# Block sums of the second layer's weights: made early and kept in DRAM instead of made where they are used

## The chip, the core and the metric

The kernel runs on one core of one Trainium2 chip. The metric is the device time of one execution in microseconds (us), lower is better. TensorE does the matrix products, VectorE and GpSimd elementwise work, ScalarE activations, copies and casts; SyncE and ScalarE start the transfers.

## The reference

Softcapped attention, followed by a two-layer network on its rows. All inputs and the output are float32.

```python
batch, n_heads, seq, head_dim = (4, 12, 448, 64)
scores = scale * np.matmul(q, k.transpose(0, 1, 3, 2))
scores = cap * np.tanh(scores / cap)
attn = softmax(scores)
x = np.matmul(attn, v)              # rows: 1792 x 768
h = x @ w_in                        # 768 x 2048
g = np.maximum(0.01 * h, h)
out = g @ w_out                     # 2048 x 768
```

(`softmax` stands for the reference's subtraction of the maximum, exponential and division by the sum.)

## The kernel before

The 1792 tokens are cut into runs of 256, 512, 512 and 512 columns. Attention goes head pair by head pair. The first two runs go through both layers as plain products, unit by unit (`plan_unit`, 34 units for each run: 16 of layer 1, then 18 of layer 2, a third of one block of 128 output columns each), while attention of later pairs is still running. The last two runs are taken together, as the two halves of a 2x2 block product with seven products in the place of eight (Winograd's form): layer 1 in eight "duos" of seven products of nine matmuls (`plan_duo`, L968), layer 2 in 7 x 3 products of 24 matmuls (`plan_product`, L1158). A float32 operand is split into a large and a small part: ScalarE or VectorE casts (L271, L275), VectorE or GpSimd subtracts (L278), and TensorE multiplies large by large, large by small, small by large.

The seven products need, of the blocks A11, A12, A21, A22 of the weights, A11, A12, A22 themselves and four sums:

```python
S1 = A21 + A22        # product 5
S2 = S1 - A11         # product 6
S3 = A11 - A21        # product 7
S4 = A12 - S2         # product 3
```

In layer 2 they are made when their turn comes, in the order `SECOND = (1, 5, 6, 7, 3, 2, 4)`, for each of three pairs p of output blocks and each half hf of the inner blocks. `plan_weights2` loads halves (256 KB) of the float32 weights, that an earlier stage left in the DRAM tiles `scratch2`, with `load_half` (L1074) into a ring of places in SBUF, and adds them with `tt2` (through `tt`, L832); S1 and S2 are kept in six places `s_home`, S3 and S4 are made in the place of the load. The finished sum is split for TensorE.

A product that adds to another's result stays in its PSUM bank. After products 1, 6 and 7 the bank is copied (L271, `keep_sum` in a duo) before the next product adds to it; after product 5 VectorE adds the bank into the output's block (L978 in a duo, L1178 in layer 2), and then product 3 adds to the bank. The banks `sc` lie in pairs in one PSUM tile (`sc_0`, `sc_1`).

The order is made by a planner (`Plan.issue`): each step has a rank, a cost per engine that may do it and the things it reads and writes. The planner takes, of the steps that are ready, the one that could begin first, then the one of lowest rank. The table `T` holds offsets by which ranks are shifted. Each engine executes its steps in the order that results, and so does each transfer queue. `raws` is the SBUF place into which the keys and queries of a quad of heads are loaded before they are transposed (`kraw`, `qraw`; L475 to L478); block operands of the last stage (`places("raws")`) take it over.

Of the kernel before, what the change touches and what calls it, by code (L numbers as in the profile page):

```python
# [9 lines left out]
F32 = mybir.dt.float32  # L10
# [45 lines left out]
    run=[576.75],
    duo=[2.07, 284.05, 910.86, -136.23, -111.69, -95.43, -23.8, -31.91],
    last=[435.37, -538.07, 227.36, -1.68, 128.15, -1225.57, -129.94, 128.6, 69.02, 131.52, 2.55, 130.66, 136.38, -656.66, 129.2, -205.76, 732.75, 763.07, -47.84, 258.93, 422.61],
    side=[-652.13, -774.99, 249.82, -374.78, 381.42, 60.8, -562.89, -191.96, 172.13, 34.67, 371.92, 318.88, -250.01, -353.24, 417.43, -547.36, -373.61, -914.07, -815.49, -153.64, -2.66, 402.24, -370.85, -380.79, -52.61, 520.81, -342.53, -165.1, -770.54, 713.99, -143.3, 356.82, -878.93, -458.23, 282.61, -767.29, 427.25, -70.55, 928.25, 302.12, -692.1, 9.97, 304.17, -205.4, -109.08, 907.85, 369.95, -402.59, -925.39, 395.77, 496.96, 41.15, 846.93, -1216.73, 1505.94, -22.9],
    phases=[(1000000000.0, {'pe': 25.03, 'dve': 0.49, 'pool': 0.13})],  # L60
# [111 lines left out]
def softcap_attention_mlp(  # L172
# [951 lines left out]
    def plan_product(idx, p, rank):  # L1124
# [58 lines left out]
        if i == 2:  # L1183
            cost, engines = {"sp": 2.1}, [nc.sync, nc.scalar]
# [150 lines left out]
```

## Time and profile before

| | us |
|---|---|
| median of three runs | 647.86 (647.61 to 649.33) |
| the profiled execution's own time | 649.59 |
| its span, first to last instruction | 647.7 |
| TensorE busy | 624.6 (96%) |
| VectorE busy | 522.3 (81%) |
| ScalarE busy | 345.6 (53%) |
| GpSimd busy | 99.2 (15%) |

The profile is one execution. An engine's busy time is what its instructions took; matmuls overlap, so a matmul's own duration (0.39 us) is longer than the step from one to the next (2.04 us for nine). Plain products and attention fill the time up to about 400 us, the duos the time to about 523 us, layer 2 of the last runs the rest up to 638.8 us, where TensorE ends; the last stores follow. Lines are those of the kernel before. In the changed kernel they are some lines further down: L278 becomes L283, L565 L570, L832 L865, L968 L1001, L1158 L1168.

### The profile page before, as it was taken

The numbers are of one execution on the slowest core, as the hardware profiler recorded it, in microseconds if no ns is written. First come the engines' busy times: TensorE is split into PE (matmuls) and PEld (weight loads), VectorE is DVE, ScalarE is ACT, GpSimd is POOL, SyncE is SP. The second block draws the span as 40 slices with busy tenths as digits, with TensorE's granted clock in tenths as the row PEclk, the third lists the DMA queues.
The fourth block names the chain that finished last, engine by engine and source line by source line (L and its number), as shares of the span: only waits on it lengthen the run. The fifth ranks groups of instructions, "written<-read, shape, count | busy, mean of one in ns | idle before, by whom it ended". The sixth has DMA issues, their size and how long they took to land.

```text
span 647.7 us, 9153 instructions
## 1 busy us (share of the span) xinstructions
PE 624.6 (96%) x3220; PEld 433.5 (67%) x3220; DVE 522.3 (81%) x834; ACT 345.6 (53%) x524; POOL 99.2 (15%) x86
## 2 busy tenths in 40 slices
PE   7899999999999999999999999999998999999994
PEld 4333655555666568677665788778887778877884
DVE  4899999999899989468675997664779999998851
ACT  4998688976867754445446244223433634564320
POOL 1032202301030322000120402010221200101100
PEclk8999999999999999999999999999999999999998
DMA  8964568859749754223232155210311275246444
GB/s 276 368 214 139 156 215 294 253 163 297 237 129 329 231 155 148 97 58 122 72 91 54 48 122 122 79 49 1 97 50 40 73 254 157 71 132 146 90 73 70
DMA packets 105254, 93.49 MB, mean 144 GB/s; under 512 B 53745, under 2 KB 84465, under 8 KB 105201
## 3 DMA queue, kind: packets, MB, share of 16 engines
q1 hardware_dynamic: 98496, 91.58, 47.6%
q10 hardware_dynamic: 6704, 1.25, 1.0%
q8 instruction: 27, 0.44, 0.3%
q14 instruction: 27, 0.21, 0.1%
HBM read 74.71 MB, written 18.09 MB: 143 GB/s over the span
## 4 chain that ended last, share of the span: by engine, by line
PE 92%; DVE 3%; ACT 3%; DMA 1%; issue 1%; SPq 0%; ACTq 0%
PE m L743 34%; PE sc L968 11%; PE sc L1158 10%; PE sc L499 9%; PE po L544 9%; PE po L1158 5%; PE po L968 4%; PE sc L496 3%; PE m L1158 3%; PE m L968 2%; PE po L519 1%; DMA raws<-in_k_dram 1%; ACT exps L554 1%; PE m L548 1%; PE po L591 1%
## 5 line engine op out<-in xcount | busy, mean ns | idle before, releaser
L743 PE MATMUL m<-bank,ws 128*128 128x256 f32 x384 | 91.6, 388 | 0.0
L271 ACT CAST w<-ws 128x384 fp32r<-128x384 f32 (+3 forms) x84 | 52.0, 626 | 71.3 <-PE m L743 19.8
L743 PEld LDWEIGHTS m<-bank,ws 128*128 128x128 f32 x384 | 70.2, 190 | 25.1 <-issue 12.2
L554 ACT ACTIVATE exps<-sc 128x896 f32<-128x896 f32 (+1 forms) x72 | 58.4, 835 | 43.1 <-PE sc L499 21.9
L278 DVE TENSOR_TENSOR w<-ws,w 128x384 fp32r<-128x384 f32 (+3 forms) x85 | 62.1, 736 | 21.4 <-ACT w L271 20.2
L499 PE MATMUL sc<-heads 32*128 32x448 f32 x576 | 66.8, 571 | 5.2 <-DVE heads L477 2.4
L743 PE MATMUL m<-bank,w 128*128 128x512 f32 x288 | 68.2, 394 | 0.0
L743 PEld LDWEIGHTS m<-bank,w 128*128 128x128 f32 x288 | 53.3, 188 | 15.8 <-issue 4.8
L557 ACT ACTIVATE exps<-exps 128x896 f32<-128x896 f32 (+1 forms) x72 | 61.0, 871 | 0.5
L743 PE MATMUL m<-xh,w 128*128 128x512 f32 x192 | 61.2, 394 | 0.0
L499 PEld LDWEIGHTS sc<-heads 32*128 32x128 f32 x576 | 27.2, 186 | 34.1 <-issue 14.4
L544 PE MATMUL po<-exps,norm 128*64 128x448 f32 x232 | 49.0, 551 | 0.0
L743 PEld LDWEIGHTS m<-xh,w 128*128 128x128 f32 x192 | 36.0, 188 | 11.1 <-issue 2.9
L278 POOL TENSOR_TENSOR w<-ws,w 128x384 fp32r<-128x384 f32 (+3 forms) x14 | 20.2, 1440 | 136.4 <-ACT w L271 84.7
L743 PE MATMUL m<-xl,w 128*128 128x512 f32 x96 | 37.4, 390 | 0.0
L544 PEld LDWEIGHTS po<-exps,norm 128*64 128x64 f32 x232 | 14.9, 137 | 29.1 <-issue 21.3
L688 DVE SCALAR_TENSOR_TENSOR bank<-bank 128x768 int32<-128x768 int32 (+1 forms) x34 | 32.5, 960 | 1.8 <-ACT ws L686 1.6
L686 ACT ACTIVATE ws<-bank 128x768 f32<-128x768 f32 (+1 forms) x34 | 29.8, 879 | 6.2 <-PE m L743 4.5
L691 DVE SCALAR_TENSOR_TENSOR ws<-ws,bank 128x768 int32<-128x768 int32 (+1 forms) x34 | 30.3, 896 | 0.3
L1158 PE MATMUL sc<-exps,w 128*128 128x512 f32 x114 | 28.6, 390 | 0.8 <-DVE bank L1178 0.8
L680 ACT ACTIVATE bank<-bank 128x768 int32<-128x768 uint8 (+1 forms) x27 | 23.7, 876 | 5.6 <-DMA bank<-in_moe_w_out_dram 4.2
L1158 PEld LDWEIGHTS sc<-exps,w 128*128 128x128 f32 x114 | 21.3, 188 | 5.6 <-DVE bank L1178 1.2
(229 smaller groups left out, 1186.6 us busy)
## 6 DMA issues: line engine op xcount, KB each, us to landing
ws<-scratch SPq DMA_DIRECT2D x38, 384.0 KB, 3.2
bank<-in_moe_w_in_dram SPq DMA_DIRECT2D x16, 768.0 KB, 7.4
scratch<-ws SPq DMA_DIRECT2D x22, 384.0 KB, 4.3
ws<-scratch SPq DMA_DIRECT2D x28, 256.0 KB, 3.6
raws<-in_k_dram SPq DMA_DIRECT2D x12, 448.0 KB, 5.9
bank<-scratch SPq DMA_DIRECT2D x20, 256.0 KB, 3.6
raws<-in_q_dram SPq DMA_DIRECT2D x11, 448.0 KB, 5.8
norm<-in_v_dram SPq DMA_DIRECT2D x48, 96.0 KB, 3.5
```

Of the source, the lines that this page charges most:

```text
L271: nc.scalar.copy(o, i)
L278: ENG[eng].tensor_tensor(out=o, in0=a, in1=f32(b), op=ALU.subtract)
L499: nc.tensor.matmul(sc[r // 2][:, r % 2, 0:S], keys(a)[part4[r], x, P * g:P * g + P], queries(c)[part4[r], x], **flags)
L544: nc.tensor.matmul(at("po", 2 * i)[half[j], 0:S], at("vc", i)[:, j, g], pf(g)[:, j if wide(g) == 2 else 0], start=(g == 0), stop=(g == NG ...
L554: a = plan.add(r, {"act": ct}, lambda e, sc=sc, g=g: nc.scalar.activation(pf(g), sc(), AF.Tanh, scale=scale_of["tanh"]), vers("sc", [g]) + ...
L557: plan.add(r + 2, {"act": ct + 0.03}, lambda e, g=g: nc.scalar.activation(pf(g), pf(g), AF.Exp, scale=scale_of["exp"]), (), vers("pf", [g] ...
L686: b = plan.add(rank, {"act": ca}, lambda e: nc.scalar.activation(ws(), word(1).bitcast(F32), AF.Abs, scale=2.0 ** -112), [("wr", m)], [("w ...
L688: a = plan.add(rank, {"dve": cv}, lambda e: nc.vector.scalar_tensor_tensor(out=word(1), in0=word(1), scalar=-0x80000000, in1=word(0), op0= ...
L691: plan.add(rank, {"dve": cv}, lambda e: nc.vector.scalar_tensor_tensor(out=z(), in0=z(), scalar=3, in1=word(1), op0=ALU.logical_shift_left ...
L743: nc.tensor.matmul(ps(), l, r, start=begins and some[0] == 0 and i == 0, stop=ends and some[-1] == len(cs) - 1 and i == len(ops) - 1)
L968: nc.tensor.matmul(ps(), l, r, start=start and x == 0, stop=x == len(ops) - 1, skip_group_check=not start)
L1158: nc.tensor.matmul(ps()[:, lo:hi], l, r[:, lo:hi], start=start and n0 == 0 and x == 0, stop=n0 == NK - 2 and x == len(ops) - 1, skip_group ...
```

## The change

The four sums are made in an earlier stage. `plan_sums` is called for 24 cells x: pair p of output blocks (3) and inner block n (8). It loads the four 128x128 blocks of its cell, two at a time, into a third of the raw keys' part of `raws`, makes the four sums in place, and stores the cell to new DRAM tiles `sums2`. The planner may give the additions to VectorE or GpSimd. The cell's loads wait for the last quad's transposes or for the store of the cell three before; the block operands that take `raws` over later wait for the last three cells' stores. `plan_weights2` then has one load of 256 KB per product, pair and half, of a sum from `sums2` or of plain blocks from `scratch2`, and no addition. The places `s_home` are now free, and hold the transposed output of product 2 before its stores, where the ring `ot` did. The table of offsets has new numbers throughout.

```diff
@@ T
+    ps=245,
+    pd=4.5,
...
+    wholes = {}
...
+        wholes[name] = whole
...
+    KEPT = (6, 3, 7, 5)
+    sums2 = [dram.tile([P, 4, 4 * P], F32, name=f"sums2_{s}") for s in range(2 * NPQ)]
+    plan.ring("pre", 3)
...
+    def plan_sums(x, rank):
+        plan.part("sum", "", x)
+        p, n = divmod(x, K4)
+        cell = wholes["raws"][:, 4 * P * (x % 3):4 * P * (x % 3) + 4 * P].rearrange("p (i f) -> p i f", f=P)
+        A11, A12, A21, A22 = ((lambda j=j: cell[:, j]) for j in range(4))
+        freed = [(t, n_quads - 1) for t in ("kraw", "qraw")] if x < 3 else []
+        for row in range(2):
+            e_ = 2 * p + row
+            plan.add(rank - T["wl"], {"sp": 0.65}, lambda e, row=row, e_=e_: nc.sync.dma_start(out=cell[:, 2 * row:2 * row + 2], in_=scratch2[e_][:, n:n + K4 + 1:K4]),
+                     [(f"scratch{NF + NCH * e_ + c}", 0) for c in range(NCH)], [("pr", 2 * x + row)], xfer=0.45, freed=freed if x < 3 else [("pre", x - 3)])
+        cost = {"dve": 0.07 + 1.04e-3 * P, "pool": 0.15 + 2.35e-3 * P}
+        done_ = []
+        for o, a, b, op in ((A22, A21, A22, ADD), (A21, A11, A21, SUB), (A11, A22, A11, SUB), (A12, A12, A11, SUB)):
+            done_ = [tt(rank, o, a, b, op, [("pr", 2 * x), ("pr", 2 * x + 1)], [("pre", x)], cost=cost, after=done_)]
+        plan.add(rank + 2, {"sp": 0.65}, lambda e: nc.sync.dma_start(out=sums2[2 * p + n // 4][:, :, P * (n % 4):P * (n % 4) + P], in_=cell),
+                 [("pre", x)], [("p2", x)], xfer=0.85)
...
+        if name == "raws":
+            over = [("pre", x) for x in range(NF // 2 * NPQ - 3, NF // 2 * NPQ)]
...
-        if i == 5:
-            load_half(1, 0, p, hf, rank, sums, ("S0", s), s_home[s][1])
-            q_, v_ = load_half(1, 1, p, hf, rank)
-            tt2(rank, sums, sums, q_, ADD, [("S0", s), v_], ("S1", s))
-            src, reads = sums, [("S1", s)]
-        elif i == 6:
...
+        if i in KEPT:
+            src, reads = load_half(rank, lambda: sums2[s][:, KEPT.index(i)], [("p2", K4 * p + 4 * hf + k) for k in range(4)])
         else:
...
+            src, reads = load_half(rank, lambda: scratch2[e_][:, lo:lo + 4].rearrange("p c f -> p (c f)"), [(f"scratch{NF + NCH * e_ + c}", 0) for c in range(NCH)])
...
         if i == 2:
-            cost, engines = {"sp": 2.1}, [nc.sync, nc.scalar]
+            cost, engines, ver, freed = {"sp": 2.1}, [nc.sync, nc.scalar], ("oz", 20 + p), s_home[3 + p][1]
+            buf = lambda: s_home[3 + p][0]().rearrange("p (s d) -> p s d", d=32)
...
+    for x in range(K4 * NPQ):
+        plan_sums(x, T["ps"] + T["pd"] * x)
```

What the instructions' order shows, at three places. First TensorE at the end of duo 5 and the start of duo 6 (`po_1` is the bank that duo 5's products 5 and 3 share, `po_0` that of its products 1, 6, 7, 4; `sc_0<-xl` begins duo 6). Before:

```order
L968 MATMUL po_1_82<-exps_2_2530,w_2_1669 128x512 x3
L968 MATMUL po_1_82<-norm_2_2620,w_2_1669 128x512 x6
L968 MATMUL po_0_81<-bank_8_2_2128,w_2_1669 128x512 x3
L968 MATMUL po_0_81<-bank_9_2_2161,w_2_1669 128x512 x4
L968 MATMUL po_0_81<-bank_10_2_2213,w_2_1669 128x512
L968 MATMUL po_0_81<-bank_9_2_2161,w_2_1669 128x512
L968 MATMUL po_1_82<-norm_2_2620,w_2_1669 128x512 x7
```

Now:

```order
L1001 MATMUL po_1_82<-exps_2_2728,w_2_1675 128x512 x3
L1001 MATMUL po_1_82<-norm_2_2803,w_2_1675 128x512 x6
L1001 MATMUL po_0_81<-bank_8_2_2247,w_2_1675 128x512 x3
L1001 MATMUL po_0_81<-bank_9_2_2279,w_2_1675 128x512 x4
L1001 MATMUL po_0_81<-bank_10_2_2368,w_2_1675 128x512
L1001 MATMUL po_0_81<-bank_9_2_2279,w_2_1675 128x512
L1001 MATMUL sc_0_79<-xl_89,w_2_1675 128x512 x9
L1001 MATMUL po_1_82<-norm_2_2803,w_2_1675 128x512 x7
```

Duo 6's first product has moved between the two products on `po_1`.

Second GpSimd during the plain products (L565 and L570, L562 and L567 are softmax sums, L278 and L283 subtractions of splits, L865 the new sums). Before:

```order
L562 TENSOR_TENSOR norm<-exps 128x896
L565 TENSOR_TENSOR norm<-norm,exps 64x448
L278 TENSOR_TENSOR w_1669<-ws,w_1669 128x768
L278 TENSOR_TENSOR raws_1727<-wait,raws_1727 128x512
L565 TENSOR_TENSOR norm<-norm,exps 64x448
L278 TENSOR_TENSOR w_1669<-ws,w_1669 128x768
L278 TENSOR_TENSOR bank_2_1912<-g_103,bank_2_1912 128x512
```

Now:

```order
L567 TENSOR_TENSOR norm<-exps 128x896
L570 TENSOR_TENSOR norm<-norm,exps 64x448 x2
L283 TENSOR_TENSOR w_1675<-ws,w_1675 128x768
L865 TENSOR_TENSOR raws<-raws 128x128 x19
L570 TENSOR_TENSOR norm<-norm,exps 64x448
L865 TENSOR_TENSOR raws<-raws 128x128 x4
L283 TENSOR_TENSOR bank_2_1921<-g_103,bank_2_1867 128x512
L865 TENSOR_TENSOR raws<-raws 128x128 x61
L567 TENSOR_TENSOR norm<-exps 128x896
L865 TENSOR_TENSOR raws<-raws 128x128 x12
```

All 96 additions are on GpSimd, with three other instructions between them.

Third ScalarE at the end (casts of weights `w_2`, and the stores of product 2 from `ot` before, from `norm` now, which ScalarE starts in turn with SyncE). Before:

```order
L271 CAST raws_2_1727<-wait_90 128x512
L271 CAST w_2_1669<-bank_10_3_3594 128x512 x2
L708 DMA out_dram<-ot_0_105 32x4x32 x2
L708 DMA out_dram<-ot_0_105 32x12x32 x2
L708 DMA out_dram<-norm_3_3611 32x4x32 x2
L708 DMA out_dram<-norm_3_3611 32x12x32 x2
```

Now:

```order
L276 CAST raws_2_2600<-wait_90 128x512
L276 CAST w_2_1675<-bank_10_3_3771 128x512
L713 DMA out_dram<-norm_3_3797 32x4x32 x2
L713 DMA out_dram<-norm_3_3797 32x12x32 x2
L276 CAST w_2_1675<-bank_10_3_3771 128x512
L713 DMA out_dram<-norm_3_3797 32x4x32 x2
L713 DMA out_dram<-norm_3_3797 32x12x32 x2
L276 CAST w_2_1675<-bank_10_3_3771 128x512
```

The casts of the last weights now stand behind four stores each.

## Rows read from the trace of the kernel before

**Rows 1.** Five stretches: from:to and length, each engine's busy us, granted clock, DMA share, GB/s.

```profile
core 0: us, PE busy (x) PEld busy (x) DVE busy (x) ACT busy (x) POOL busy (x), PEclk, DMA share, GB/s
...
240.00:360.00 120.00, 120.00 (x600) 83.19 (x600) 84.27 (x117) 56.24 (x81) 15.32 (x9) 1.00 0.31 91
480.00:520.00 40.00, 37.41 (x164) 30.37 (x163) 37.59 (x59) 17.80 (x34) 9.70 (x7) 1.00 0.22 66
520.00:560.00 40.00, 38.49 (x167) 30.94 (x167) 39.34 (x63) 20.26 (x36) 4.09 (x2) 1.00 0.56 171
560.00:600.00 40.00, 38.54 (x169) 31.23 (x168) 36.27 (x62) 19.63 (x36) 2.95 (x2) 1.00 0.51 130
600.00:648.00 48.00, 38.76 (x194) 32.89 (x192) 23.37 (x36) 9.36 (x16) 4.27 (x3) 0.95 0.45 75
```

**Rows 2.** TensorE's waits, 395 to 648 us: for whom, us in total, times, longest.

```profile
PE po L968 <- DVE bank L978: 1.7, 1, 1.7
PE sc L968 <- ACT bank L271: 1.4, 2, 0.7
PE sc L968 <- DVE wait L978: 0.9, 1, 0.9
PE sc L968 <- DVE xh L978: 0.9, 1, 0.9
PE sc L1158 <- DVE bank L1178: 0.8, 1, 0.8
PE sc L1158 <- ACT bank L271: 0.7, 1, 0.7
PE sc L1158 <- DVE wait L978: 0.7, 1, 0.7
```

**Rows 3.** The chain that ended last, 395 to 648 us: start, us, what.

```profile
408.59 0.59 ACT bank L271
...
487.64 2.33 PE po L968 x9
489.97 2.04 PE sc L968 x9
```

**Rows 4.** Line 832, 515 to 610 us: eight of the 24 sums, ns min/median/max.

```profile
L832 DVE TENSOR_TENSOR norm<-norm,ws x8: 680/686/687, 529.2 to 546.2; 128x512 f32<-128x512 f32 x8
```

**Rows 5.** GpSimd's instructions by shape: count, busy us, mean ns, idle before.

```profile
L278 POOL TENSOR_TENSOR w<-ws,w 128x384 fp32r<-128x384 f32 x7 | 8.4, 1196 | 31.2 <-ACT w L271 21.9 <-PE po L968 6.5 <-DMA ws<-scratch 1.4
...
L278 POOL TENSOR_TENSOR xl<-norm,xh 128x192 fp32r<-128x192 f32 x6 | 4.3, 718 | 15.4 <-DVE xh L275 12.7 <-ACT xh L271 2.7
...
L386 POOL MEMSET norm<- 128x128 f32 x2 | 0.3, 205 | 0.0
```

**Rows 6.** Instructions in order of time, 484 to 487 us: start, us, engine, line.

```profile
484.43 1.20 POOL L278 TENSOR_TENSOR w<-ws,w 128x384 fp32r<-128x384 f32 x1 [1.42 <-DMA ws<-scratch]
484.68 1.36 DVE L278 TENSOR_TENSOR w<-g,w 128x384 fp32r<-128x384 f32 x1
...
486.43 0.55 DVE L278 TENSOR_TENSOR w<-ws,w 128x384 fp32r<-128x384 f32 x1
```

**Rows 7.** VectorE's instructions by shape, 240 to 360 us, columns as in Rows 5.

```profile
L278 DVE TENSOR_TENSOR w<-ws,w 128x768 fp32r<-128x768 f32 x16 | 16.7, 1050 | 0.2
...
L278 DVE TENSOR_TENSOR bank<-g,bank 128x512 fp32r<-128x512 f32 x15 | 10.4, 690 | 3.5 <-ACT bank L271 3.2
L565 DVE TENSOR_TENSOR norm<-norm,exps 64x448 f32<-64x448 f32 x7 | 6.2, 893 | 2.7 <-ACT exps L557 2.6
...
L278 DVE TENSOR_TENSOR w<-ws,w 128x640 fp32r<-128x640 f32 x6 | 4.9, 825 | 3.2 <-ACT w L271 2.8
...
L563 DVE TENSOR_TENSOR norm<-norm,exps 128x896 f32<-128x896 f32 x4 | 4.3, 1077 | 0.0
```

**Rows 8.** Instructions in order of time at the end, 618 to 648 us.

```profile
624.59 2.60 ACTq L708 DMA_DIRECT2D out_dram<-ot  x4
...
627.23 0.62 ACT L271 CAST raws<-wait 128x512 fp32r<-128x512 f32 x1 [3.78 <-DMA out_dram<-ot]
...
633.36 9.72 SPq L708 DMA_DIRECT2D out_dram<-norm  x14
...
638.80 0.45 DVE L1167 STREAM_TRANSPOSE norm<-po 128x256 f32<-128x256 f32 x1 [2.15 <-PE po L1158]
```

More of the change, by code (lines that the diff above doesn't have):

```diff
@@ L56 @@
[L56 to L59, printed above, removed]
@@ new lines @@
+    run=[16.57],
+    duo=[330.89, 486.97, 1747.73, -211.67, 48.39, 108.12, 114.85, 478.0],
+    last=[694.33, -552.1, 302.56, 229.54, 261.67, -1251.14, -394.06, -46.46, 1454.11, 271.52, -887.99, 762.71, -422.01, -185.91, 872.64, -981.3, 1478.44, 649.25, -136.75, 640.51, 1013.89],
+    side=[12.81, -328.49, -49.06, -1062.95, 509.42, 262.73, -964.23, -55.46, 439.0, 361.48, 573.73, 395.1, -646.04, -245.17, 769.91, 676.77, 305.52, -862.54, -1734.86, -689.43, 235.24, 495.8, -783.61, -439.02, -267.55, 909.49, -398.82, -193.61, -490.73, 618.92, -471.78, 627.09, -1389.69, -775.61, 401.34, -804.47, 684.13, 380.74, 835.71, 700.02, -796.53, -65.17, 33.36, -58.57, -37.58, 414.87, 723.61, 669.19, -2712.06, 1065.07, -238.9, -713.14, 1524.95, -1959.16, 1872.4, -53.24],
@@ L1069, in softcap_attention_mlp, with load_half @@
     n_loads = [0]
-    s_made = {}
-    tt2 = lambda rank, o, a, b, op, reads, ver, after=(): tt(rank, o, a, b, op, reads, [ver], after=after)
-    def load_half(row, col, p, hf, rank, dest=None, ver=None, freed=()):
-        e_ = 2 * p + row
-        if dest is None:
-            x = n_loads[0]
-            n_loads[0] += 1
-            dest, ver = q_home[x % NQ][0], ("wq", x)
-            freed = [(t, x - NQ) for t in ("wq", "wz")] if x >= NQ else q_home[x][1]
-        lo = NK * col + 4 * hf
-        plan.add(rank - T["wl"], {"sp": 0.65}, lambda e: nc.sync.dma_start(out=dest().rearrange("p (c f) -> p c f", f=P), in_=scratch2[e_][:, lo:lo + 4]),
-                 [(f"scratch{NF + NCH * e_ + c}", 0) for c in range(NCH)], [ver], xfer=0.85, freed=freed)
-        return dest, ver
+    def load_half(rank, source, reads):
+        x = n_loads[0]
+        n_loads[0] += 1
+        dest, ver = q_home[x % NQ][0], ("wq", x)
+        plan.add(rank - T["wl"], {"sp": 0.65}, lambda e: nc.sync.dma_start(out=dest(), in_=source()), reads, [ver], xfer=0.85,
+                 freed=[("wq", x - NQ)] if x >= NQ else q_home[x][1])
+        return dest, [ver]
     def plan_weights2(idx, p, hf, rank):
@@ L1088, in plan_weights2 @@
         s = 2 * p + hf
[L1089 to L1110 removed]
+        if i in KEPT:
+            src, reads = load_half(rank, lambda: sums2[s][:, KEPT.index(i)], [("p2", K4 * p + 4 * hf + k) for k in range(4)])
+        else:
+            row, col = {1: (0, 0), 2: (0, 1), 4: (1, 1)}[i]
+            e_, lo = 2 * p + row, NK * col + 4 * hf
+            src, reads = load_half(rank, lambda: scratch2[e_][:, lo:lo + 4].rearrange("p c f -> p (c f)"), [(f"scratch{NF + NCH * e_ + c}", 0) for c in range(NCH)])
         slot = x % NW2
@@ L1118, in plan_weights2 @@
                      if w_size * (j // 2 % T["w"]) < W2 * slot + W2 and W2 * slot < w_size * (j // 2 % T["w"] + 1)]
-        s_made[s] = split(rank + 0.5, lambda: w_half2(x)[:, 0], lambda: w_half2(x)[:, 1], src, W, reads, [("uh", x)], [("ul", x)], freed=freed)
+        split(rank + 0.5, lambda: w_half2(x)[:, 0], lambda: w_half2(x)[:, 1], src, W, reads, [("uh", x)], [("ul", x)], freed=freed)
     w_half2 = lambda x: w_all()[:, W2 * (x % NW2):W2 * (x % NW2) + W2].rearrange("p (a c) -> p a c", a=2)
@@ L1180, in plan_product @@
         reads = [("yz", NPQ * int(b_) + p)]
-        plan.add(r, {"dve": turn(W) + 0.05}, lambda e: nc.vector.transpose(out=at("ot", o).rearrange("p s d -> p (s d)"), in_=src()), reads, [("ot", o)], port=False)
-        cost, engines = {"sp": 4.2}, None
+        cost, engines, buf, ver, freed = {"sp": 4.2}, None, lambda: at("ot", o), ("ot", o), ()
         if i == 2:
-            cost, engines = {"sp": 2.1}, [nc.sync, nc.scalar]
-        plan.add(r + 1, cost, store(lambda: at("ot", o), run, 2 * p + row, engines), [("ot", o)], (), xfer=1.8, port=False)
+            cost, engines, ver, freed = {"sp": 2.1}, [nc.sync, nc.scalar], ("oz", 20 + p), s_home[3 + p][1]
+            buf = lambda: s_home[3 + p][0]().rearrange("p (s d) -> p s d", d=32)
+        plan.add(r, {"dve": turn(W) + 0.05}, lambda e: nc.vector.transpose(out=buf().rearrange("p s d -> p (s d)"), in_=src()), reads, [ver], freed=freed, port=False)
+        plan.add(r + 1, cost, store(buf, run, 2 * p + row, engines), [ver], (), xfer=1.8, port=False)
     def plan_second(rank):
```

31 lines of the change are left out of this document (10 added, 21 removed).

## The prediction

> **What bounds the kernel now.** I read the stretches first [rows 1], then TensorE's waits after 395 us [rows 2], then the chain that ended last [rows 3]. In 240 to 360 us TensorE is busy for all of 120.00 us, at the full granted clock (1.00, so 2.4 GHz): nothing there can be won, only lost. From 480 us on it misses 2.59, 1.51 and 1.46 us per 40, and VectorE is what is full: 37.59, 39.34 and 36.27 of 40. The waits of [rows 2] name it: in eight waits TensorE stands 7.1 us, five times for VectorE (5.0 us) and three times for a copy on ScalarE (2.1 us). Each wait costs a little more than it says: the nine matmuls behind the longest took 2.33 us, the next nine 2.04 [rows 3], so 0.3 us is added per restart. Eight waits are 7.1 + 8 x 0.3 = 9.5 us, and that is all that the last 240 us have to give, besides the tail: the last 48 us hold 38.76 us of TensorE.
>
> **The change, part by part.**
>
> *Sums that go from the last stage.* Of each half of weights four sums fall away: 6 halves x 4 = 24 adds of 128x512. All 24 stood on VectorE at 0.686 us [rows 4]: 16.5 us of the 113.2 us that it works in 480 to 600 us. Nothing on TensorE waits for such an add by itself; what it buys is that VectorE's other work comes earlier. 54 loads become 42.
>
> *Sums that are added.* 24 cells of 4 adds of 128x128, in the order all 96 on GpSimd, between the second unit of the second run and the twenty-second, so roughly in 240 to 345 us. No add of that size is in the trace. From below a clearing of 128x128 on GpSimd, which reads nothing, took 0.205 us; from above the subtraction of 128x192 took 0.718 [rows 5]. The line through 192 columns (0.718) and 384 (1.196) gives 0.718 - 64 x 0.00249 = 0.56 us; I take that: 53.8 us, between 19.7 and 68.9. GpSimd works 15.32 of those 120 us now [rows 1], so it has room. Each cell's four adds wait for one another, in one engine's queue, and nothing of the plain products waits for them.
>
> *What the adds do to VectorE.* While GpSimd works from 484.43 for 1.20 us, a VectorE subtraction of 384 columns lasts 1.36 us that lasts 0.55 when alone [rows 6]: it ended with GpSimd's. So VectorE's work of that kind and GpSimd's add up. The five largest such groups of the stretch are 42.5 us [rows 7]; with 53.8 for the adds and the 15.3 of GpSimd that are there already this is 111.6 of 120 us. It fits, with 8.4 to spare, so I cost it at nothing. The cover is those 8.4 us and the weights that are split up to four units ahead. Bounds: nothing, and with 0.718 us per add 126.7 of 120, so 6.7 us too much. The Trainium skill (SBUF — State Buffer, section "SBUF: two separate sides") says that VectorE with two SBUF inputs and GpSimd take turns at one pair of ports, and that the loser stands still for the whole of the other's instruction. That speaks against this change; the 1.36 us agree with it.
>
> *Transfers that are added.* 48 loads of 128 KB and 24 stores of 256 KB, 12.6 MB. The stretch moves 91 GB/s x 120 us = 10.9 MB now, at 0.31 of the DMA engines [rows 1]; at the same price per byte it becomes 0.67. SyncE's queue gets 72 issues; at 0.69 us (14 in 9.72 [rows 8], a full queue, so an upper price) they are 50 of 120 us. A store that waits for GpSimd stands ahead of the next unit's weight load, and so do the loads into a cell that is not yet stored. Those weights are wanted up to four units later, so nothing is charged; the bound is in the rival below.
>
> *The order of products.* The plain stage keeps its product order nearly, and 120.00 of 120 us leave no gain: 0. Among the block products I look, for each of the eight waits, at what stands between in the new order.
> - 487.64 us (VectorE, 1.7 us): duo 5's products 5 and 3 share a bank, and the second waits until VectorE has taken the first. One product (9 matmuls, 2.04 us) stood between them; now two do, so 2.04 us more against 1.7. Gone.
> - The wait near 505 us for `wait` (0.9) and near 521 us for `xh` (0.9): the same pair for duos 6 and 7, with 9 and 30 matmuls between its products before, 18 and 42 now. Gone.
> - Second layer, ScalarE (0.7) and VectorE L1178 (0.8): no matmul between before, now 6 and 12. Gone.
> - The two ScalarE copies of the first duos (1.4 together): unchanged.
> - A new one: duo 6 now has its pair of products in the two halves of one PSUM tile with nothing behind, as duo 0 has, where the copy waited for the second product and TensorE for the copy, from 408.59 us for 0.59 us [rows 3]. 0.7 + 0.3 = +1.0.
> - L1158 on `wait` (0.7): VectorE's add for duo 7 reads one half of a PSUM tile, the second layer's product 1 writes the other. The add now stands behind the first piece of that product and before the second, with no matmul between: it costs what the L1178 case did, 0.8. +0.1.
>
> Sum: -(1.7 + 0.9 + 0.9 + 0.7 + 0.8) - 5 x 0.3 + 1.0 + 0.1 = -5.4 us. VectorE's queue is reordered too, and a result that comes late there is a new wait; it is bounded by 0 and by the 6.5 us that the five waits cost now. I take the commonest single wait, +1.0, as VectorE has 16.5 us less to do.
>
> *The tail.* The last 28 stores leave from 633.36 us on over two queues, 14 in 9.72 us: the queues are what ends last, and not TensorE [rows 8]. The new order ends the last two products of block 2 later: the second of them leaves 5 halves of a split product (0.72 us each) and two pieces of 1.36 behind it, 6.3 to 7.0 us. On ScalarE, four stores stand ahead of the cast of weights that product 19 needs; four stores held ScalarE for 2.60 us, and the next cast started right behind them [rows 8]. So: the first of the two products ends 9.8 us before TensorE does, its stores hold ScalarE from 8.2 to 5.7 before the end, cast and subtraction take to 4.4, and the transpose of the other block stands behind them on VectorE: its 28 stores start some 3.7 us before the end, where they started 638.80 - 633.36 = 5.4 before it. +1.7 us. TensorE itself waits some 0.8 us there, which the full queues hide. Bounds: 0, if the stores are issued faster, and 3.
>
> *The start.* The first 46 us have the same products in the same order; ScalarE has the same number of other jobs between the exponentials: 0, give or take 1.
>
> **Sum.** -5.4 + 1.0 + 1.7 = -2.7 us. The profiled execution took 649.59 us, with a span of 647.7, 1.7 over the median of three runs (647.86); so 646.9 for such an execution, and **645.2 us** for a median. About 0.3% (1.9 us) is what a measurement of this kernel can tell from no change.
>
> **The rivals.**
> 1. *The adds do not fit* (chance 0.18, slower). GpSimd's adds shut out VectorE in 240 to 345 us, splits and epilogues of plain products come late, and a stage without a gap gets gaps. It decides where an add, with what it waits for, passes (120 - 42.5 - 15.3) / 96 = 0.65 us. At 0.718 the excess is 6.7 us: 645.2 + 6.7 = 651.9. For it: the 1.36 us of [rows 6], and SyncE's queue, in which stores that wait stand ahead of weights. Against it: VectorE idles 35.7 of the 120 us. The rule of the Trainium skill that I named (SBUF — State Buffer, "SBUF: two separate sides") is this rival's mechanism.
> 2. *The waits only move* (0.27, no change). VectorE's queue stays nearly full (113 - 16 of 120 us), and the reordered queue makes as many late results as the order of products removes: -5.4 + 3.5 + 1.7 = -0.2, so 647.7. For it: in 480 to 520 us, before any of the removed adds runs, VectorE is at 37.59 of 40 already, and three of the five waits that I call gone lie at its end or just before.
> 3. *All of it is won* (0.15, within faster): no new wait and no dearer tail, -5.4: 642.5. Against it: the cast behind four stores.
> 4. *The sums do not run beside the plain products at all*, because the raw keys' place comes free too late: the last transpose of the keys would have to be late. Under 0.03; I leave it in the slower part.
>
> **How the numbers follow.** Forecast 0.40 and rival 3 with 0.15 make 0.55 for faster; rival 2 0.27; rival 1 with 4 0.18. The forecast's own range is 642.5 to 647.0 (a late wait more or less, the tail's bounds). The range for all reaches down to rival 3 with a better start, 641.5, and up to rival 1 short of its far end, 650.8.
>
> **What would show it.** Right: TensorE without a wait in 240 to 360 us; adds on GpSimd at 0.46 to 0.65 us; in 480 to 600 us VectorE down by some 16 us; waits after 395 us at four or five, two of them the copies near 409 and 424 us, one near 500 for duo 6; the last stores starting under 4.5 us before TensorE's end. Wrong: waits of TensorE on VectorE casts or subtractions in 240 to 345 us (rival 1), or seven or more waits after 480 us (rival 2).

## The result, and the profile after

The changed kernel took 651.04 us (median of five runs, 650.49 to 652.41), the kernel before 647.61 in five runs beside it: ratio 1.0055, 95% interval 1.0036 to 1.0074. It is slower by half a per cent, on the other side of the forecast and 0.2 us beyond its range. The profiled execution took 650.49 us, its span is 648.7.

The five stretches of [rows 1], in the kernel after:

```profile
240.00:360.00 120.00, 119.99 (x596) 83.76 (x594) 84.94 (x112) 60.53 (x88) 62.08 (x101) 1.00 0.71 197
480.00:520.00 40.00, 39.33 (x174) 32.21 (x172) 34.16 (x58) 17.65 (x33) 10.73 (x8) 1.00 0.25 73
520.00:560.00 40.00, 38.44 (x169) 31.23 (x168) 36.60 (x61) 21.16 (x39) 1.10 (x1) 1.00 0.41 115
560.00:600.00 40.00, 40.00 (x178) 33.14 (x177) 27.45 (x45) 17.91 (x32) 4.20 (x3) 1.00 0.45 106
600.00:648.00 48.00, 33.68 (x172) 28.64 (x170) 18.76 (x32) 7.58 (x13) 5.27 (x4) 0.90 0.42 70
```

Nothing is lost beside the plain products: TensorE is busy 119.99 of 120 us, with GpSimd at 62 in place of 15 us and twice the transfers. In 480 to 600 us VectorE works 98.2 us where it worked 113.2. In the last 48 us TensorE works 5.1 us less than before: it is done earlier. Its waits after 395 us, against [rows 2]:

```profile
PE sc L1001 <- ACT bank L276: 1.4, 2, 0.7
PE sc L1168 <- DVE wait L1011: 0.8, 1, 0.8
PE sc L1001 <- DVE xh L1037: 0.8, 1, 0.8
PE sc L1001 <- ACT xh L276: 0.7, 1, 0.7
```

Five waits of 3.7 us are left of eight of 7.1. So TensorE did win what was forecast, and the loss comes behind it. The two queues that start stores, from 611 us (SyncE) and 619 us (ScalarE), in order of time (start, us, engine and line, how many), against [rows 8]:

```profile
611.77 4.35 SPq L713 DMA_DIRECT2D out_dram<-ot  x8
616.22 4.98 SPq L713 DMA_DIRECT2D out_dram<-norm  x4
621.61 6.96 SPq L713 DMA_DIRECT2D out_dram<-ot  x8
628.67 15.46 SPq L713 DMA_DIRECT2D out_dram<-norm  x22
```

```profile
619.16 1.81 ACTq L713 DMA_DIRECT2D out_dram<-norm  x4
624.06 0.62 ACT L276 CAST w<-bank 128x512 fp32r<-128x512 f32 x1 [9.27 <-DMA out_dram<-ot]
625.42 1.86 ACTq L713 DMA_DIRECT2D out_dram<-norm  x4
627.38 0.62 ACT L276 CAST w<-bank 128x512 fp32r<-128x512 f32 x1 [2.70 <-DMA out_dram<-norm]
629.38 8.59 ACTq L713 DMA_DIRECT2D out_dram<-norm  x14
```

Before, both queues had 14 stores left at 633.36 us and were done together. Now ScalarE has 14 left at 629.38 and has started its last by 637.97; SyncE has 22 left at 628.67 and has started its last by 644.13. For six microseconds SyncE alone starts stores. It also stood still between stores: what SyncE's queue waited for from 606 us (us, times, longest) is

```profile
SPq L713 <- DMA out_dram<-norm: 11.7, 8, 3.4
```

that is, for the landing of stores that ScalarE had mostly started itself. Before, it was 2.3 us in six waits: 0.5 in two for stores from `norm`, 1.8 in four for those from `ot`, where product 2's output was. A semaphore is a counter that one instruction raises and another waits for. The trace's records of the transfers name the semaphore of each: in both kernels there are eight, taken strictly in turn over both queues, and a transfer waits until the one eight places ahead of it has landed, whichever queue that is in. So a SyncE store whose data are ready can stand behind one that ScalarE starts late: SyncE's plain store at 611.77 us shares its semaphore with the store that ScalarE started at 608.73, one turn ahead.

The time, split at the first duo matmul and at TensorE's end (us; "behind" is from there to the end of the span):

| execution | first duo | block products | TensorE's end | behind | span |
|---|---|---|---|---|---|
| before, as shown | 400.2 | 238.5 | 638.8 | 8.9 | 647.7 |
| before, a second one (e_before) | 399.4 | 238.4 | 637.8 | 7.2 | 645.0 |
| after | 399.6 | 234.1 | 633.7 | 15.0 | 648.7 |
| a_even | 399.6 | 234.6 | 634.2 | 9.8 | 644.0 |
| a_three | 399.7 | 234.1 | 633.8 | 8.8 | 642.6 |
| a_last | 399.6 | 234.1 | 633.7 | 13.1 | 646.9 |
| a_swap | 399.6 | 234.1 | 633.7 | 15.7 | 649.4 |
| a_sync15 | 399.7 | 234.1 | 633.8 | 17.9 | 651.7 |
| a_ot | 399.6 | 234.1 | 633.7 | 9.8 | 643.5 |
| a_tail | 400.2 | 235.7 | 635.9 | 13.1 | 649.0 |
| a_ring | 399.6 | 238.7 | 638.3 | 9.4 | 647.7 |
| a_order | 399.8 | 241.7 | 641.5 | 7.2 | 648.7 |
| b_order | 399.4 | 246.5 | 645.8 | 8.9 | 654.7 |
| b_noadds | 399.5 | 239.1 | 638.6 | 7.6 | 646.2 |

Block products: 4.5 us won. Behind them: 6.1 us lost against the execution shown, 7.8 against the second.

### The profile page after: what moved, and what is told of

The parts are those of the page before. It is cut to its first block, busy times and chain, and to the rows that moved or that the text cites. A ratio compares the mean times of both kernels' runs of the same rounds, so it can differ in the third digit from the quotient of the medians.

```text
span 648.7 us, 9319 instructions
## 1 busy us (share of the span) xinstructions
PE 624.5 (96%) x3220; PEld 435.2 (67%) x3220; DVE 505.6 (78%) x812; ACT 350.3 (54%) x530; POOL 141.7 (22%) x174
## 4 chain that ended last, share of the span: by engine, by line
PE 94%; ACT 2%; DMA 1%; DVE 1%; issue 0%; SPq 0%
PE m L748 34%; PE sc L1001 12%; PE sc L1168 10%; PE sc L504 10%; PE po L549 9%; PE po L1168 5%; PE po L1001 4%; PE sc L501 3%; PE m L1168 3%; PE m L1001 3%; PE po L524 1%; DMA raws<-in_k_dram 1%; ACT exps L559 1%; PE m L553 1%; PE po L596 1%; ACT w L559 0%
## 5 line engine op out<-in xcount | busy, mean ns | idle before, releaser
L276 ACT CAST w<-ws 128x384 fp32r<-128x384 f32 (+3 forms) x92 | 57.7, 634 | 70.1 <-PE m L748 26.5
L283 DVE TENSOR_TENSOR w<-ws,w 128x384 fp32r<-128x384 f32 (+3 forms) x95 | 69.5, 740 | 22.5 <-ACT w L276 21.0
L865 POOL TENSOR_TENSOR raws<-raws 128x128 f32<-128x128 f32 x96 | 54.7, 583 | 33.4 <-DMA raws<-scratch 29.8
L562 ACT ACTIVATE exps<-exps 128x896 f32<-128x896 f32 (+1 forms) x72 | 61.1, 871 | 0.7
L283 POOL TENSOR_TENSOR w<-ws,w 128x384 fp32r<-128x384 f32 (+2 forms) x11 | 15.1, 1376 | 89.8 <-ACT w L276 86.3
```

Of the source, the lines that this page charges most:

```text
L276: nc.scalar.copy(o, i)
L283: ENG[eng].tensor_tensor(out=o, in0=a, in1=f32(b), op=ALU.subtract)
L562: plan.add(r + 2, {"act": ct + 0.03}, lambda e, g=g: nc.scalar.activation(pf(g), pf(g), AF.Exp, scale=scale_of["exp"]), (), vers("pf", [g] ...
L865: return plan.add(rank, cost, lambda e: ENG[e].tensor_tensor(out=o(), in0=a(), in1=b(), op=op), reads, writes, after=after, freed=freed, p ...
```

## The experiments

Ratios are to the kernel before on the same chip, with 95% intervals; the changed kernel's is 1.0055.

**The kernel before again (e_before)**

> The kernel before, unchanged, for a second profile and for the noise. If the execution shown first was slow at its start only (granted clock 0.5 in 12.1 to 15.5 us), this one has its first duo matmul about 1 to 2 us before 400.2 us, TensorE's end near 637 and the same 8.9 us from there to the end of the span. If the start is the same here, the median of the kernel before has to be explained in another way. Ratio 1.000 +- 0.002.

647.90 us, 1.0009 (0.9996 to 1.0022). Its profiled execution starts the duos 0.85 us earlier than the one shown first (mean granted clock in the first 50 us 1.00 there, 0.97 in the first), and needs 1.7 us less behind TensorE. So the spans differ by 1.0 us and the medians by 3.4: the execution shown ahead of the prediction was a long one.

**Even queues (a_even)**

```diff
-cost, engines, ... = {"sp": 4.2}, None, ...
+cost, engines, ... = {"sp": 4.2}, [nc.sync, nc.scalar] if i == 3 and p else None, ...
```

> The changed kernel; the eight stores of the second and third block of product 3 are started by SyncE and ScalarE in turn, where SyncE started all eight. Every engine else has the same order. Theory 1 (SyncE's queue of stores is what ends last: ScalarE's last store is issued at 638.0, SyncE's at 644.1, 11 of them alone): 8 issues of 0.5 us less on SyncE, the last issue near 640.5, so about 3.5 us less than the changed kernel, 647.5. Theory 2 (the recorded one: ScalarE is held by stores, and casts of the last weights come late): 8 triggers more on ScalarE make it worse, 652 or more.

645.79 us, 0.9968 (0.9957 to 0.9979): 5.25 us less than the changed kernel, and faster than the kernel before. Both queues have 18 stores left from 625.9 us and end together; SyncE's queue from 606 us and ScalarE's last stores:

```profile
SPq L713 <- DVE norm L1195: 4.4, 1, 4.4
SPq L713 <- DVE norm L1177: 4.3, 3, 2.3
...
SPq L713 <- DMA out_dram<-norm: 1.0, 4, 0.3
```

```profile
629.95 9.44 ACTq L713 DMA_DIRECT2D out_dram<-norm  x14
```

SyncE now waits more for data than for landings (all landings: 5.8 us, 3.2 of them of loads, in place of 13.5; those of stores from `norm` 1.0 in place of 11.7). By an estimate the eight starts fewer are worth 8 x 0.5 = 4 us; this run changes the waits together with the number, and does not part the two. More starts on ScalarE did TensorE little harm (0.5 us).

**The order of the last products (a_tail)**

```diff
+        fixed = [...]
...
             for n, t in ready.items():
+                if n in fixed and n != fixed[0]:
+                    continue
...
             del ready[n]
+            if n in fixed:
+                fixed.remove(n)
```

> The changed kernel; the last 24 pieces of TensorE's products are in the order of the kernel before, everything before them as it was; SyncE's order is the same. Theory 3 (the order of the last products is what makes the end dear, since products 16 and 17 end 5 to 10 us later than before): the time from TensorE's end to the end of the span goes back from 15.0 to about 9, 645. Theory 1 (SyncE's queue has too much in it whatever the order of products): SyncE's waits for stores that ScalarE issues get shorter, but its last issue stays within 2 us of 644, 649 to 651.

650.80 us, 1.0047 (1.0029 to 1.0064). TensorE ends 2.2 us later and the kernel as late as the changed one: SyncE's last 22 stores run from 627.41 for 17.01 us, to 644.42 (644.13 in the changed kernel). What TensorE does last does not set the end. Theory 3 falls.

**Two stores change places (a_swap)**

```diff
-            s["fn"](eng)
+            seq.append((n, eng))
...
+        place = {n: k for k, (n, _) in enumerate(seq)}
+        late = seq.pop(place[2140])
+        seq.insert(place[2098], late)
+        for n, eng in seq:
+            steps[n]["fn"](eng)
```

> The changed kernel in its own order, with as many stores on either queue; only the store of product 15 and that of product 13 change places, so that SyncE's eight of 13 stand ahead of the four and four of 15. If the number of stores on SyncE is what counts: 650 to 652. If it is the waits of SyncE for the landing of stores that ScalarE starts late (10.6 us in the changed kernel): up to 3 us come back, 648.

651.15 us, 1.0050 (1.0032 to 1.0067); SyncE's waits for landings of stores from `norm` are 13.8 us. That order is not the cause.

**The last stores on ScalarE (a_last)**

```diff
-store(buf, run, 2 * p + row, [nc.sync, nc.scalar], (lo, hi))
+store(buf, run, 2 * p + row, [nc.sync, nc.scalar] if p == 0 or p == 2 and not lo else [nc.scalar], (lo, hi))
```

> The changed kernel in its own order; product 19 and the second half of product 20 are stored by ScalarE alone (12 stores), where both queues had six each. If part of the end is that SyncE alone has 11 stores left when ScalarE has none (638.0 to 644.1): SyncE's last issue comes 6 x 0.48 = 2.9 us earlier, 648. If the end is only the waits of SyncE for the landing of ScalarE's stores, ScalarE's queue becomes the late one and it stays at 650 to 652.

648.77 us, 1.0011 (0.9999 to 1.0023): 2.3 us less than the changed kernel by the medians, 2.9 by the ratios. SyncE's waits for landings of stores from `norm` stayed (15.0 us). So 2 to 3 us of the loss are the uneven end; the rest lies ahead of it.

**One more store on SyncE alone (a_sync15)**

```diff
-cost, engines, ver, freed = {"sp": 2.1}, [nc.sync, nc.scalar], ("oz", 20 + p), ...
+cost, engines, ver, freed = {"sp": 2.1}, [nc.sync, nc.scalar] if p else None, ("oz", 20 + p), ...
```

> The changed kernel in its own order; the store of product 15 (the first block of product 2) is started by SyncE alone, eight stores where it had four. Coupling: SyncE's wait of 3.5 us near 608 us, for the landing of ScalarE's half of this store, goes, against 4 x 0.5 us of added starts: 649 to 651. Number alone: 2 us more, 653.

653.49 us, 1.0073 (1.0059 to 1.0087): 2.4 us more than the changed kernel by the medians, 1.2 by the ratios, whose intervals overlap. It is not faster, as the waits alone would have made it; that the number counts by itself is not shown. The wait near 608 us did go, but only to the next store of ScalarE's, near 613 to 621 us; SyncE's waits from 606 us:

```profile
SPq L713 <- DMA out_dram<-norm: 13.0, 4, 7.4
```

So this run does not part the two causes as I had thought: the queue stands until that store lands.

**The places of product 2's output (a_ot, a_ring)**

a_ot changes `buf` alone, so that the order stays that of the changed kernel. a_ring tells the planner too, and keeps TensorE's order by a_tail's edit with a longer list:

```diff
+if i == 2:
+    buf, ver, freed = lambda: at("ot", o), ("ot", o), ()
```

> The changed kernel in its own order; the transposed output of product 2 goes to the ring of two places, as in the kernel before, in place of the places that the sums left. If these places are of use to the end: VectorE's transposes wait for the landing of the eight stores before them, which come late in SyncE's queue, 652 to 656. If not: 651 +- 0.7.

> The changed kernel with TensorE's whole order as it is; only the transposed output of product 2 goes to the ring of two places again, as in the kernel before, and the planner orders its transposes and stores by that. As many stores on SyncE as in the changed kernel. Coupling (the new places let ScalarE's half of a store come ahead of its turn, and SyncE's older stores wait for it): the end comes some 4 us earlier, 647, with SyncE's waits for landings of ScalarE's stores at 3 us in place of 12. Number of stores alone: 650 to 652.

a_ot: 647.10 us, 0.9983 (0.9971 to 0.9995), below both expectations; in its order, made for other places, some stores find a later block in their place, so that parts of the output are other blocks' values. For the queues it is the clearest run all the same. Each of them starts the same stores in the same order as in the changed kernel, and TensorE ends at 633.7 us in both; but behind it a_ot needs 9.8 us in place of 15.0. What differs is the turn at the semaphores: ScalarE's first store of product 2 stands among the second eight plain stores of SyncE and not among the first eight, and starts at 612.30 us and not at 608.73. SyncE's waits for landings from 606 us are 3.3 us in place of 13.5:

```profile
SPq L713 <- DMA out_dram<-ot: 1.7, 3, 0.8
SPq L713 <- DMA out_dram<-norm: 1.6, 4, 0.6
```

So the number of SyncE's stores, and their order in its queue, need not make a long end.

a_ring, with an order of its own: 649.95 us, 1.0021 (1.0012 to 1.0030). It is outside the expectation for the coupling: the time is 3 us longer, and SyncE's waits for landings are 9.2 us where 3 were expected, 7.7 of them in one wait ahead of 624 us. Behind TensorE's end it needs 9.4 us in place of 15.0, as the queues run level after that, but 4.6 us of it are lost on TensorE. In order of time, 626 to 630 us:

```profile
626.28 1.87 ACTq L728 DMA_DIRECT2D out_dram<-ot  x4
628.53 1.14 ACT L291 CAST w<-bank 128x512 fp32r<-128x512 f32 x2 [13.72 <-DMA out_dram<-ot]
...
629.20 2.16 PE L1183 MATMUL po<-xl,w 128*128 128x256 f32 x7 [2.55 <-ACT w L291]
```

A cast of the last weights stands on ScalarE behind four stores, whose transpose on VectorE had stood 6.40 us until earlier stores had landed. TensorE waits 2.55 us for the cast, and runs at the lower granted clock for a while after (mean 0.89 in 618 to 634 us). The new places spare TensorE this; in the changed kernel they also let ScalarE's stores of product 2 run ahead of SyncE's (608.73 against 616.22 us for the first block, together at 612.30 in a_ot).

**The sums and the order, one at a time (b_order, a_order, b_noadds)**

b_order and a_order have a_tail's edit with longer lists; b_noadds has

```diff
-tt2 = lambda ...: tt(rank, o, a, b, op, reads, [ver], after=after)
+tt2 = lambda ...: plan.add(rank, TT, lambda e: None, reads, [ver], after=after)
```

> The kernel before, sums and all, with TensorE's block products in the changed kernel's order from the first duo to the last 24 pieces, which keep the order of before; the planner orders the other engines around it. Theory O (the order of products alone takes the waits away): four or five waits after 395 us as in the changed kernel, block products 4.4 us shorter, 643.2. Theory S (it is VectorE's load, the 24 additions of 16.5 us, that made the waits): seven or more waits stay, 647 to 649.

> The changed kernel, with its early sums, with all of TensorE's block products in the order of the kernel before; the planner orders the other engines around them. Theory S (the sums taken from VectorE shorten the block products in either order): TensorE's end at 634 or 635 in place of 638, with five or six waits after 395 us. Theory O (the waits go with the order of the products, and the sums only make that order possible): the eight waits of before stay, TensorE's end near 638. In both the order of the stores is near that of before, so that the time behind TensorE's end is 7 to 10 us: 644 by S, 647.5 by O.

> The kernel before in its own order, instruction by instruction, without the 24 additions of the second layer (products 5, 6, 7 and 3 multiply by unsummed weights); the loads stay. Theory S: with 16.5 us less on VectorE in 515 to 600 us its results come earlier and waits go: 643 to 645. Theory O: all waits before 525 us are there as they were, and of the two behind 560 us one at most is shorter: 646.5 to 648.

b_order 656.65 us, 1.0138 (1.0119 to 1.0158); a_order 650.49, 1.0037 (1.0024 to 1.0050); b_noadds 647.38, 0.9987 (0.9977 to 0.9998). TensorE's waits from 395 us in b_order:

```profile
PE sc L1173 <- DVE w L293: 5.0, 3, 3.6
PE sc L1173 <- DVE exps L293: 1.4, 1, 1.4
PE sc L983 <- ACT bank L286: 1.4, 2, 0.7
PE sc L1173 <- ACT w L286: 1.2, 1, 1.2
PE sc L1173 <- DVE wait L993: 0.8, 1, 0.8
PE sc L983 <- DVE xh L1019: 0.8, 1, 0.8
PE sc L983 <- ACT xh L286: 0.7, 1, 0.7
...
```

The five waits of the changed kernel are all here and those that it removed are gone: that is the order's doing. But new waits of 8 us stand beside them, mostly for splits of weights and of block operands that VectorE has not made yet. Without the additions and in the old order (b_noadds), the eight waits stay: the room alone gives 0.1%. With the sums early and the old order (a_order), TensorE waits ten times and the block products take 241.7 us. So neither half alone gave more than 0.1% here; b_order and a_order came out above what either theory allowed. In b_order and a_order the other engines were ordered by ranks made for other products, so that the 8 and 3 us that they lose are not the price of the missing half alone.

**The sums twice (a_double)**

```diff
-done_ = [tt(rank, o, a, b, op, ..., cost=cost, after=done_)]
+done_ = [plan.add(rank, cost, lambda e, ...: [ENG[e].tensor_tensor(out=o(), in0=a(), in1=b(), op=op) for _ in range(2)], ..., after=done_)]
```

> The changed kernel in its own order; each of the 96 additions on GpSimd is made twice (the sums become others). GpSimd would have to work about 115 of the 105 us in 240 to 345. The recorded rival 1, that GpSimd's additions shut VectorE out and plain products wait: gaps of TensorE in 240 to 360 us, 5 us or more over the changed kernel. My reading of the changed kernel's trace, that VectorE's work beside GpSimd's is only 0.1 to 0.2 us longer an instruction and has 30 us to spare: no gap, the sums are ready some 10 to 20 us later, 651 +- 1.

685.33 us, 1.0579 (1.0556 to 1.0602): my reading was wrong. What rival 1 forecast, gaps in the plain products, is there as soon as the room is used up, though not on the engine that it named. First the stretches 240 to 345 and 345 to 395 us (columns as in [rows 1]), then TensorE's waits in both, then SyncE's in the first:

```profile
240.00:345.00 105.00, 92.01 (x400) 67.59 (x399) 58.45 (x73) 42.87 (x65) 88.18 (x149) 0.92 0.54 159
345.00:395.00 50.00, 42.88 (x206) 23.96 (x204) 29.13 (x40) 17.59 (x24) 30.23 (x49) 0.90 0.56 140
```

```profile
PE m L748 <- DVE g L772: 12.4, 3, 5.8
PE po L596 <- DVE rs L592: 4.5, 1, 4.5
PE po L549 <- DMA norm<-in_v_dram: 2.3, 1, 2.3
...
```

```profile
SPq L830 <- POOL raws L828: 50.9, 15, 6.2
```

VectorE is not full (58 of 105 us). Two queues are held instead. On GpSimd the few other jobs stand behind additions, here the subtraction that ScalarE and VectorE wait for ahead of TensorE's first gap (in order of time, 276 to 279 us):

```profile
276.47 1.26 POOL L283 TENSOR_TENSOR bank<-g,bank 128x512 fp32r<-128x512 f32 x1
...
277.76 0.60 ACT L767 ACTIVATE g<-m 128x512 f32<-128x512 f32 x1 [8.87 <-POOL bank L283]
...
278.39 0.69 DVE L772 TENSOR_TENSOR g<-m,g 128x512 f32<-128x512 f32 x1 [3.81 <-ACT g L767]
```

And on SyncE the store of each cell waits for GpSimd, 50.9 us in all, with the weights of later units behind it. The changed kernel's own row is

```profile
SPq L829 <- POOL raws L865: 13.4, 13, 3.5
```

which costs TensorE nothing. The duos begin 34.2 us later; TensorE's waits there are 20.2 us, and the granted clock of 0.92 and 0.90 accounts for most of the rest (105 x 0.08 + 50 x 0.10 = 13.4).

**The kernel before with even queues (b_even)**, the edit of a_even

> The kernel before; the stores of the second and third block of product 3 are started by SyncE and ScalarE in turn. Both queues are level there already at 633 us and SyncE waits for data ahead of that, so by theory 1 nothing is to be won: ratio 1.000 +- 0.002. If alternate starting is worth 3 us by itself, whatever the order, 644.5.

647.52 us, 0.9994 (0.9983 to 1.0005). Where the queues are level, there is nothing to win.

**A third queue (a_three, a_ring3)**

```diff
-store(buf, run, 2 * p + row, [nc.sync, nc.scalar], (lo, hi))
+store(buf, run, 2 * p + row, [nc.sync, nc.scalar, nc.gpsimd] if p else [nc.sync, nc.scalar], (lo, hi))
```

> The changed kernel with the even queues, and the stores of products 19 and 20 started by SyncE, ScalarE and GpSimd in turn (5 of 20 by GpSimd, which idles there). If the starting of stores is what ends last: 14 starts a queue become 11 or 12, about 1.5 us less than with two even queues, 644. If the landing of the stores or GpSimd's slower start decides: no gain over 645.8, or a loss of up to 2.

> a_ring with the stores of products 19 and 20 started by SyncE, ScalarE and GpSimd in turn. By coupling and the starting of stores together: 645, near the 644.4 of the even queues with a third.

a_three has a_even's edit besides. It takes 644.38 us, 0.9943 (0.9927 to 0.9958), the best of all: 3.8 us under the kernel before and 6.7 under the changed one. GpSimd's stores, in order of time:

```profile
630.09 1.25 POOL L713 DMA_DIRECT2D out_dram<-norm  x2 [4.23 <-DVE norm L1177]
632.67 1.17 POOL L713 DMA_DIRECT2D out_dram<-norm  x2 [1.33 <-DVE norm L1177]
634.55 0.58 POOL L713 DMA_DIRECT2D out_dram<-norm  x1 [0.71 <-DVE norm L1177]
```

a_ring3: 649.41 us, 1.0006 (0.9997 to 1.0016), where 645 was expected: TensorE's wait for the cast is there as in a_ring, and the 0.5 us gained on it is not clear of the noise.

## Why the prediction was wrong, and where it was right

**Block products: right.** Forecast -5.4 + 1.0 = -4.4 us, measured 238.5 to 234.1, so -4.5. The waits came out nearly one by one: the pairs of duos 5 and 6 and the two of the second layer are gone, the two copies near 408 and 423 us unchanged, the new one for duo 6 there (0.7, at 495.6 us), the one for `wait` at 0.8. At 521 us nothing was won: TensorE stands ahead of the same product of duo 7 as before (0.78 us, before 0.85), now for VectorE's last step on product 4's block (L1037) and not for the add after product 5. The late wait that I allowed for without a place covers it; that it fell there is luck. What the sums have to do with it I had not said well: the order removes the waits (b_order), and the room on VectorE by itself does not (b_noadds). That the order needs this room is argued, not shown, as b_order's new waits may come from the ranks of its other engines.

**Sums beside plain products: right that they fit.** 583 ns for an addition on the mean (estimate 0.56 us), no gap:

```profile
L865 POOL TENSOR_TENSOR raws<-raws 128x128 f32<-128x128 f32 x96 | 54.7, 583 | 33.4 <-DMA raws<-scratch 29.8
```

That the mean meets the estimate is in part luck: half of the additions took 463 ns or less, the longest 1192. VectorE's neighbours, the first row from before and the others from after, against [rows 7]:

```profile
L767 DVE TENSOR_TENSOR g<-m,g 128x512 f32<-128x512 f32 x16 | 11.0, 687 | 1.5 <-ACT g L762 1.3
L283 DVE TENSOR_TENSOR w<-ws,w 128x768 fp32r<-128x768 f32 x17 | 17.9, 1057 | 0.8 <-ACT w L276 0.6
L283 DVE TENSOR_TENSOR bank<-g,bank 128x512 fp32r<-128x512 f32 x15 | 12.8, 854 | 1.4 <-ACT bank L276 1.4
L772 DVE TENSOR_TENSOR g<-m,g 128x512 f32<-128x512 f32 x16 | 11.0, 689 | 10.2 <-ACT g L767 10.1
```

The subtraction of 512 columns with both inputs in SBUF went from 690 to 854 ns; the maximum that reads a PSUM bank did not change (687, 689). The Trainium skill (SBUF — State Buffer, section "SBUF: two separate sides") has VectorE with two SBUF inputs and GpSimd take turns at one pair of ports. The trace agrees in part: of the five groups of [rows 7] three became longer, but the largest, of 768 columns, hardly changed (1050 to 1057 ns), and one became shorter (893 to 814). If 463 ns is an addition that is left alone, the longer ones cost GpSimd 96 x (0.583 - 0.463) = 11.5 us, by that estimate, against 15 x 0.16 = 2.5 us on VectorE's subtraction of 512 columns. In [rows 6], too, I had read more than is there: VectorE's subtraction did not end with GpSimd's but 0.4 us behind it (486.04 against 485.63). Rival 1 was put on VectorE; what gives way first are GpSimd's own queue and SyncE's, of which I had named the second beside it (a_double).

**The tail: wrong, and this decides.** The step that failed is "The last 28 stores leave ... over two queues, 14 in 9.72 us", carried over to the new order as "its 28 stores start some 3.7 us before the end ... +1.7 us". ScalarE's 14 did start 4.3 us ahead of TensorE's end. But SyncE had 22 left by then. I counted only the stores that begin last, and not what stood in SyncE's queue ahead of them: the plain stores of product 3, eight a block and all on SyncE, whose last eight run from 621.6 to 628.6 us in the new order, and the queue's waits for ScalarE's stores. The tail became 15.0 us and not 8.9 + 1.7 = 10.6; with even queues (a_even) it is 9.8, and the median 645.79, 0.6 us from the forecast. The Trainium skill (Perfetto Trace Analysis, section "DMA Optimizations") says that balancing transfers over the engines that can start them may help where making their descriptors is the limit. In a_even and a_three it did help, by 5.25 us and a further 1.4; that descriptors are the limit here no run shows. ScalarE's casts behind four stores, which I had given as the cause, cost TensorE nothing in the changed kernel; they do in a_ring.

**The places for product 2** I had left out of the sum, without a reason. They are worth 4.6 us on TensorE and cost 5.6 us behind it (a_ring against the changed kernel).

**The start: right**, 399.6 us for the first duo matmul, between 399.4 and 400.2 before.

How SyncE's waits and the number of its stores share the blame is not fully settled. a_ot speaks for the waits: with every store in its old queue, 5.2 us of the end go when the turn at the semaphores is another; but part of its output is other blocks' values. a_last gives 2.9 us to the uneven end alone, a_even both together; a_sync15 shows that one wait taken away comes back at the next.

## What to carry to other kernels

A tail that ends in stores is a queue, and has to be costed as one: for each queue, list what is left in it at the point where the last data are ready, in order, with what each waits for; two queues that were level in the old order need not be in the new. Where transfers of several queues share a fixed set of semaphores in turn, a queue with ready work stops behind a late transfer of another. Room on a full engine need not pay by itself (0.1% in b_noadds): look for the waits that it would shorten. And work that is hidden at one size can be dear at twice the size (a_double).

## What was not expected of the hardware

Starting a store from GpSimd took 0.6 us, no more than from SyncE or ScalarE (9.44 / 14 = 0.67 us in a full queue), and the third queue gave 1.4 us. And TensorE's granted clock fell to its lower level (1.2 GHz) for part of the stretches in which it had gaps of 2 to 6 us (0.92 and 0.90 on the mean in a_double), so that gaps cost more than their length: 34.2 us for 20.2 us of waits.
